# PSUM's eight banks as one pool, one argmax chain per head pair, and a new order of the attention stage

## The chip, the cores and the metric

The kernel runs on one core of one Trainium2 chip. Its time is the device time of that core, in microseconds, from the launch to the end of the last engine. Before the change the median of three runs is 634.14 us (634.08 to 634.79).

## The reference

Three blocks follow each other. Only the first, a clustered attention, is touched by the change; the other two are named since they fill the rest of the time.

```python
# attention: B=2, H=8, S=768, D=64, 16 clusters per head
q_assign = argmax(q_n @ c_n.T)          # cluster of every query (normalised rows)
k_assign = argmax(k_n @ c_n.T)          # cluster of every key
mask = q_assign[:, None] == k_assign[None, :]
scores = where(mask, q @ k.T / 8, -1e9)
attn = exp(scores - max(scores)); attn /= sum(attn) + 1e-9
x = attn @ v                            # heads side by side: (B, S, 512)
# block 2: xk, xr = mixes of x and x shifted by one token
x = sigmoid(xr @ w_r) * (relu(xk @ w_k) ** 2 @ w_v)
# block 3: token mixing, then channel mixing
u = x + (relu(x.T @ w_tok1) @ w_tok2).T
out = u + relu(u @ w_ch1) @ w_ch2
```

## The kernel before

**Tiling.** Heads are worked two at a time: eight pairs, numbered 0 to 7. A pair has 12 tasks: two token halves (hf 0 and 1) of three 128-query tiles for each of the two heads (e 0 and 1). One task is: scores of 128 queries against 768 keys (`score`, four TensorE matmuls of 384 columns, tile `s`, two PSUM banks); the row maximum (`rowmax`, VectorE); the exponential (`expo`, ScalarE, tile `e`); then a turn of `e`, because attn @ v needs keys on the partitions. Tasks of half 0 are turned on TensorE (`transp_p`, six transposes of 128 columns in two groups of three, tile `t`, and two copies out of PSUM by VectorE or ScalarE, `evac_p`); tasks of half 1 are turned in 32x32 blocks on VectorE (`transp_d`) and put in place by 16 DMAs per pair (`shuffle`, tile `ptd`). The product with v (`pv`) is a chain of 12 matmuls for a half, accumulated in one bank (tile `x`; the trace records every such plain float32 matmul twice, so 24 rows a chain); `xevac` scales it by the reciprocal row sums, which `denom`, `recip`, `spread`, `rbcast` (three transposes, tile `rb`) and `rbevac` bring to the right partitions.

**Mask.** While pair n is worked, pair n+1 is prepared: q and k are split into a high and a low part (`hi`, `lo`), and the clusters are found. `sims` multiplies q and k with the centroids; `sime` copies that to SBUF, for each half of the tokens apart (128x384); `simt` turns each half with three TensorE transposes; `amx`, `aeq`, `ark`, `am2`, `aoh` (VectorE, 128x192 each) make a one-hot row of the first maximum; `mask` turns it back (three transposes) and `mske` (ScalarE) scales it. So there are two chains of these steps per pair, one per half. `mdma` then moves the result by four DMAs on SyncE's queue into rows of the q and k operands, where the second part of every score matmul adds it; no score of pair n+1 can start before.

**PSUM.** Eight banks are dealt out by name: `psS` holds two score tiles of two banks each, `psT` two banks for turned tiles, `pair` one bank `m` (sims, masks, row sums) and one bank `x` (the v product, the other half of sims). When attention ends, these pools are closed and six accumulators `a0` to `a5` for the blocks behind take their place, beside `x` and `m`.

**What sets the order.** Within the attention stage a planner in the kernel's own Python code (`Op`, `run_plan`) places every operation. Each `Op` has an engine, an assumed duration, its predecessors, and a due time from the tables `DUE`, `EARLY` (pair 0) and `LATE` (the last pair). At every step the planner takes, over all engines, the ready operation that can start first, with due times as the tie-breaker at a weight of `DUE_W`. On the chip each engine then runs its list strictly in that order. A score op of task g waits in the plan for `exp_` of task g-2, since there are two score tiles. Where TensorE would pause at the start, `fill_x` puts 14 idle transposes. After the attention stage a second scheduler (`Chain`, `pump`) lays out the dense blocks; its rules are not touched.

Of the kernel before, what the change touches and what calls it, by code (L numbers as in the profile page):

```python
# [33 lines left out]
SCALE = 1.0 / math.sqrt(D)  # L34
NSTG = 3
# [21 lines left out]
DUE = {'s': 0.075,  # L57
 'mx': -0.216,
 'ex': 0.934,
 'td': 1.972,  # L60
 'tp0': 2.127,
 'tp1': 1.924,
 'ev0': 2.789,
 'ev1': 2.471,
 'sime0': 3.215,
 'simt0': 3.916,
 'amx0': 3.075,
 'aeq0': 4.244,
 'ark0': 0.056,
 'am20': 5.655,  # L70
 'aoh0': 5.222,
 'mask0': 6.793,
 'mske0': 7.102,
 'sime1': 5.354,
 'simt1': 4.15,
 'amx1': 6.062,
 'aeq1': 3.912,
 'ark1': 3.439,
 'am21': 2.284,
 'aoh1': 4.612,  # L80
 'mask1': 7.092,
 'mske1': 6.0,
 'mdma': 11.061,
 'hi00': 4.779,
 'hi01': 3.762,
 'hi02': 1.798,
 'hi10': -5.56,
 'hi11': 7.343,
 'hi12': 9.268,
 'lo00': 4.909,  # L90
 'lo01': 6.659,
 'lo10': 7.645,
 'lo11': 13.069,
 'loads': 11.015,
 'loadv': 22.198,
 'rcp': 8.118,
 'rbp': 9.821,
 'rep': 12.198,
 'rcd': 12.255,
 'rbd': 13.951,  # L100
 'red': 15.747,
 'pvd': 20.878,
 'pvp': 12.812,
 'xed': 22.451,
 'xep': 13.571,
 'ksp': 0.283,
 'ksd': 0.542,
 'sh': 15.329,
 'sims': 3.038,
 'f0': -2.206,  # L110
 'f1': 1.08,
 'f2': -0.163,
 'f3': 0.286,
 'f4': 0.039,
# [11 lines left out]
EARLY = {0: {'simt1': 6.854,
     'f1': -0.046,
     'lo01': 6.792,
     'lo11': 11.641,
     'amx1': 6.029,  # L130
     'rep': 11.63,
     'sh': 14.421,
     'loadv': 23.651,
     'mske0': 4.694,
     'xed': 22.706,
     'g': 12.575,
     'sime1': 4.215,
     'rcd': 10.132,
     'mask1': 6.301,
     'ark0': 3.08,  # L140
     'f6': -2.983,
     'hi02': 3.667,
     'rcp': 6.686,
     'pvd': 20.92,
     'am20': 5.3,
     'lo00': 5.616,
     'ksp': -0.992,
     'f8': 0.942,
     'loads': 12.84,
     'x1': 10.466,  # L150
     'rbd': 14.022,
     'tp1': 1.876,
     'ksd': 0.54,
     'f9': 1.924,
     'aeq1': 4.212,
     'xep': 12.88,
     'simt0': 2.943,
     'x0': 2.453,
     'ev1': 2.379,
     'mask0': 7.408,  # L160
     'hi01': 3.184,
     'mske1': 6.134}}
# [68 lines left out]
def cluster_attention_moe_mixer(ctx: ExitStack, tc, q, k, v, cent, mu_k, mu_r, w_k, w_v, w_r, w1, w2, wc1, wc2, out):  # L231
# [15 lines left out]
    nc.vector.tensor_copy(identb, ident)  # L247
    rank = const.tile([P, NC], F32, name="rank")
# [271 lines left out]
    with ExitStack() as actx:  # L520
# [4 lines left out]
        pctx = actx.enter_context(ExitStack())  # L525
        psS = pctx.enter_context(tc.tile_pool(name="psS", bufs=2, space=PSUM))
        psT = pctx.enter_context(tc.tile_pool(name="psT", bufs=2, space=PSUM))
# [27 lines left out]
        def prep_steps(n):  # L555
# [29 lines left out]
            def sims():  # L585
                for hf in range(2):
                    st["ps", hf] = pair.tile([P, HS], F32, tag="mx"[hf], name="sims")
                for e in range(2):
                    for j, r in ((0, qr), (1, kr)):
                        o = 32 * (2 * e + j)  # L590
                        for hf in range(2):
                            rows = slice(D * hf, D * hf + D)
                            nc.tensor.matmul(
                                st["ps", hf][o : o + 32, :], cn[rows, 2 * p + e, :],
                                r[e][rows, hf * HS : (hf + 1) * HS], start=True, stop=True,
                            )

            def sims_head(e):
                if e:
                    st["ps", e] = ps = psT.tile([P, HS], F32, tag="t", name="sims")  # L600
                else:
                    st["ps", e] = ps = pair.tile([P, HS], F32, tag="m", name="sims")
# [28 lines left out]
            def sime(hf):  # L631
                sm = sml.tile([P, HS], F32, tag="sm", name="sm")
                nc.scalar.activation(sm, st["ps", hf], AF.Copy)
                st["sm", hf] = sm
# [849 lines left out]
```

## Time and profile before

| | |
|---|---|
| median of 3 runs | 634.14 us (634.08 to 634.79) |
| profiled execution | span 633.0 us from first to last instruction; no own time is listed for it beside the span |
| TensorE busy (PE) | 618.0 us, 98% |
| VectorE busy (DVE) | 484.3 us, 77% |
| ScalarE busy (ACT) | 358.9 us, 57% |
| GpSimd busy (POOL) | 129.2 us, 20% |
| mean granted TensorE clock | 0.995 |

The median lies 1.1 us above the span of the profiled execution. A busy TensorE is not a TensorE at its peak: matmuls are pipelined, and a row's duration holds the time in the pipe, so that rows overlap. What an instruction costs the stream is read from the distance between the start of its row and the start of the next. SPq is SyncE's DMA queue, PEld TensorE's weight loads. In the 40 slices of the page (15.8 us each) attention fills the first 15.

### The profile page before, as it was taken

To read this page: it belongs to the slowest core of one execution; us is meant where nothing else is said; L and a number is where in the kernel's file an instruction comes from. 1 tells how busy PE (TensorE), PEld (TensorE's weight loads), DVE (VectorE), ACT (ScalarE), POOL (GpSimd) and SP (SyncE) were. 2 spreads that over 40 slices of the span, in tenths; PEclk is the share of its full clock that TensorE was granted. 3 is DMA by queue.
4 is the path that set the end of the run, shared out by engine and by line. 5 is a ranking of instruction groups with operands and counts; after the bars stand their busy time and mean duration, and the time that the engine had idled before them with its cause. 6 is when DMAs were issued, how large, how long until landed. Compare 5 with 4: busy or idle time off the path is not lost.

```text
span 633.0 us, 9550 instructions
## 1 busy us (share of the span) xinstructions
PE 618.0 (98%) x3357; PEld 500.5 (79%) x3357; DVE 484.3 (77%) x888; ACT 358.9 (57%) x690; POOL 129.2 (20%) x181
## 2 busy tenths in 40 slices
PE   7899999999999999999999999999999999999997
PEld 5756657566575677899999998888999899999996
DVE  5789898999988955788969889869988635875113
ACT  4878888788886956776748665314443421332110
POOL 4354735547264351000000000020002000000000
PEclk9799999999999999999999999999999999999999
DMA  8156847749574352333312443151446312410002
GB/s 289 63 163 152 240 133 217 209 101 269 167 184 109 80 150 100 100 121 115 126 38 67 133 134 133 36 132 45 157 133 155 100 45 100 133 34 1 1 1 99
DMA packets 36735, 75.43 MB, mean 119 GB/s; under 512 B 6032, under 2 KB 19344, under 8 KB 36688
## 3 DMA queue, kind: packets, MB, share of 16 engines
q1 hardware_dynamic: 34256, 67.36, 34.7%
q0 software_dynamic: 2432, 7.47, 4.9%
q8 instruction: 26, 0.43, 0.3%
q14 instruction: 21, 0.17, 0.1%
HBM read 48.27 MB, written 3.15 MB: 81 GB/s over the span
## 4 chain that ended last, share of the span: by engine, by line
PE 76%; DVE 11%; ACT 5%; issue 3%; DMA 2%; SPq 1%; POOL 0%; DVEq 0%; ACTq 0%; POOLq 0%
PE h L1230 25%; PE acc L1254 24%; PE x L844 8%; PE s L755 6%; PE r L513 5%; DVE junk L763 3%; ACT e L772 3%; DMA uperm<-ublk 2%; PE t L828 2%; SPq L1352 1%; PE tok L1310 1%; ACT ptp L536 1%; PE tok L1393 1%; PE rb L794 1%; DVE ut L1365 1%
## 5 line engine op out<-in xcount | busy, mean ns | idle before, releaser
L1254 PE MATMUL acc<-wu,hl 128*128 128x512 f32 x720 | 170.5, 391 | 0.0
L1254 PEld LDWEIGHTS acc<-wu,hl 128*128 128x128 f32 x720 | 134.6, 188 | 26.8
L1230 PE MATMUL h<-ut,wu 128*128 128x384 f32 x576 | 104.5, 336 | 0.4 <-DVE ut L1365 0.3
L772 ACT ACTIVATE e<-s,nm 128x768 f32<-128x768 f32 x96 | 86.5, 902 | 29.8 <-DVE junk L763 26.6
L1230 PEld LDWEIGHTS h<-ut,wu 128*128 128x128 f32 x576 | 100.9, 188 | 3.0 <-DVE ut L1365 0.8
L763 DVE TENSOR_SCALAR_CACHE_REDUCE junk<-s 128x768 bf16<-128x768 f32 x96 | 90.4, 942 | 13.3 <-PE s L755 12.4
L1209 ACT ACTIVATE hl<-h 128x384 fp32r<-128x384 f32 x48 | 23.5, 491 | 93.7 <-PE h L1230 93.7
L1211 DVE SCALAR_TENSOR_TENSOR hl<-h,hl 128x384 fp32r<-128x384 f32 x48 | 26.7, 557 | 60.0 <-ACT hl L1209 59.6
L406 ACT ACTIVATE wu<-g 128x512 fp32r<-128x512 f32 x62 | 39.1, 630 | 55.9 <-DVE g L402 55.9
L1230 PE MATMUL h<-xmix,wu 128*128 128x384 f32 x384 | 69.2, 335 | 0.0
L1230 PEld LDWEIGHTS h<-xmix,wu 128*128 128x128 f32 x384 | 67.3, 188 | 1.1
L755 PE MATMUL s<-ka,qa 128*128 128x384 f32 x192 | 59.3, 391 | 3.1 <-ACT e L772 2.6
L1352 POOL DMA_DIRECT2D uperm<-ublk x16 | 7.9, 500 | 229.5 <-ACT h L1297 169.1
L755 PEld LDWEIGHTS s<-ka,qa 128*128 128x128 f32 x192 | 29.5, 193 | 29.9 <-ACT e L772 21.0
L755 PE MATMUL s<-kb,qb 80*128 80x384 f32 x192 | 50.1, 343 | 0.9 <-POOL kb L538 0.9
L408 DVE TENSOR_TENSOR wu<-g,wu 128x512 fp32r<-128x512 f32 x58 | 40.5, 698 | 13.1 <-ACT wu L406 11.4
L402 DVE SCALAR_TENSOR_TENSOR g<-wu,g 128x512 f32<-128x512 f32 x62 | 42.8, 690 | 4.5
L807 DVE STREAM_TRANSPOSE tb<-e 128x768 f32<-128x768 f32 x48 | 45.8, 959 | 0.0
L390 DVE SCALAR_TENSOR_TENSOR g<-wraw,g 128x512 uint32<-128x512 uint32 x62 | 42.7, 689 | 1.1
L828 PE MATMUL t<-ident,e 128*128 128x128 f32 x288 | 42.6, 281 | 0.7 <-DVE ptp L534 0.3
L396 DVE SCALAR_TENSOR_TENSOR g<-wraw,g 128x512 uint32<-128x512 uint32 x62 | 42.4, 684 | 0.2
L828 PEld LDWEIGHTS t<-ident,e 128*128 128x128 f32 x288 | 34.7, 144 | 7.9 <-issue 3.6
(112 smaller groups left out, 879.4 us busy)
## 6 DMA issues: line engine op xcount, KB each, us to landing
wraw<-moe_w_ch_dram SPq DMA_DIRECT2D x34, 512.0 KB, 3.5
ptd<-tb SPq DMA_DIRECT2D x88, 144.0 KB, 4.2
t<-q_dram SPq DMA_DIRECT2D x16, 384.0 KB, 4.4
t<-k_dram SPq DMA_DIRECT2D x16, 384.0 KB, 4.7
ptd<-tb POOLq DMA_DIRECT2D x40, 144.0 KB, 4.3
wraw<-moe_w_k_dram SPq DMA_DIRECT2D x9, 512.0 KB, 3.3
wraw<-moe_w_v_dram SPq DMA_DIRECT2D x9, 512.0 KB, 3.9
v<-v_dram SPq DMA_DIRECT2D x8, 384.0 KB, 3.8
```

The source lines that it names most:

```text
L390: nc.vector.scalar_tensor_tensor(out=g, in0=high, scalar=0xC0000000, in1=g, op0=ALU.bitwise_and, op1=ALU.bitwise_or)
L396: nc.vector.scalar_tensor_tensor(out=g, in0=low, scalar=29, in1=g, op0=ALU.logical_shift_right, op1=ALU.bitwise_or)
L402: nc.vector.scalar_tensor_tensor(out=gf, in0=f32(t[:, 1, :]), scalar=TINY, in1=gf, op0=ALU.is_ge, op1=ALU.mult)
L408: (nc.gpsimd if key[0] == "wr" else nc.vector).tensor_tensor(out=t[:, 1, :], in0=gf, in1=f32(t[:, 0, :]), op=ALU.subtract)
L755: nc.tensor.matmul(ps[:, nh, 0:HS], x[:, e, c0 : c0 + P], y[:, e, nh * HS : (nh + 1) * HS], start=first, stop=not first,)
L763: nc.vector.tensor_scalar(junk, PS_[t][:, :, 0:HS], -SCALE, None, op0=ALU.mult, op1=ALU.min, accum_out=nm)
L772: nc.scalar.activation(et.rearrange("p (a b) -> p a b", a=2), PS_.pop(t)[:, :, 0:HS], AF.Exp, bias=NM_.pop(t), scale=SCALE, accum_out=ss_[ ...
L807: nc.vector.transpose(out=T_[n][:, :, e, :, i, :].rearrange("p j k q -> p k j q"), in_=E_.pop(t).rearrange("p (k j c) -> p k j c", j=4, c=32),
L828: nc.tensor.transpose(ps[:, kk], E_[t][:, kt * P : (kt + 1) * P], ident)
L844: nc.tensor.matmul(o, vts[n][:, e, kt, :], m, start=(kt == 0), stop=(kt == NT - 1))
L1230: nc.tensor.matmul(ps[:, 0:HS], u[:, wl, c, :], xin(xl, c, sl), start=(n == 0), stop=(n == 11))
L1254: nc.tensor.matmul(accs[st], prev[:, xl, st * P : (st + 1) * P], u[:, wl, :], start=(idx == 1 and n == 0), stop=(idx == nf and n == 2),)
```

## The change

1. One PSUM tile `banks8` of eight banks replaces the four pools. An `Op` now says how many banks it needs (`need`) and which earlier operations' banks its end gives back (`frees`); `pick_banks` chooses the bank, and `start` makes an op wait for one. Scores take any even-odd pair of banks, single tiles any bank. The wait of a score for `exp_` of task g-2 and the waits by name of bank are gone; which operation waits for which is decided by the planner through the banks.
2. The two argmax chains per pair become one over both token halves: `sime`, `amx` to `aoh`, `mask` and `mske` run once per pair on twice the size. `simt` is no longer a transpose of 128 columns but a matmul of the same weights with `pick`, 64 columns of the identity, so that only the 16 used columns of each group of 32 are written.
3. In pair 0 the five argmax steps and one mask copy, which were one operation or stood ahead of the plan, become operations of the plan.
4. All due times are set anew, many far outside the pair (-218, 202), and with them the order on every engine. `fill_x` has no predecessor any more.
5. Behind the attention stage the six accumulators and the two small banks keep whichever banks the plan left them (`home`).

TensorE, in the second half of a pair in steady state (before: pair 2 to pair 3): the v products (`x`) of the pair before and of this pair, the scores (`s`, each task two rows `ka` and `kb`), the row sums (`rb`).

```order
L844 MATMUL x<-ptd,v_270 64x384 x4
L755 MATMUL s<-ka_635,qa_633 128x384 x2
L755 MATMUL s<-kb_636,qb_634 128x384 x2
L844 MATMUL x<-ptd,v_270 64x384 x2
L755 MATMUL s<-ka_938,qa_936 128x384 x2
L755 MATMUL s<-kb_939,qb_937 128x384 x2
L844 MATMUL x<-ptp,v_940 64x384 x4
L755 MATMUL s<-ka_938,qa_936 128x384 x2
L755 MATMUL s<-kb_939,qb_937 128x384 x2
L844 MATMUL x<-ptp,v_940 64x384 x6
```

The same place of the program after the change; every PSUM tile is called `ps` now.

```order
L843 MATMUL ps<-ptd,v_949 64x384 x4
L754 MATMUL ps<-ka_870,qa_868 128x384 x2
L754 MATMUL ps<-kb_871,qb_869 128x384 x2
L754 MATMUL ps<-ka_870,qa_868 128x384 x2
L754 MATMUL ps<-kb_871,qb_869 128x384 x2
L843 MATMUL ps<-ptd,v_949 64x384 x8
L843 MATMUL ps<-ptp,v_1121 64x384 x2
L754 MATMUL ps<-ka_1169,qa_1167 128x384 x2
L754 MATMUL ps<-kb_1170,qb_1168 128x384 x2
L793 MATMUL ps<-ident,rw 128x128 x3
```

Stretches of v matmuls are longer and fewer, and two tasks' scores stand next to each other between them. Over the whole stage the v products stand in 25 stretches where they stood in 46, and the scores in 80 where they stood in 93.

VectorE, at the argmax of the coming pair, before: the two chains with the row maxima (`junk`) between.

```order
L647 TENSOR_REDUCE mx<-simsT 128x12
L650 TENSOR_TENSOR simsT<-simsT,mx 128x12x16
L656 TENSOR_TENSOR simsT<-simsT,rank 128x12x16
L763 TENSOR_SCALAR junk,nm<-s 128x768
L662 TENSOR_REDUCE m_1466<-simsT 128x12
L665 TENSOR_TENSOR oh<-simsT,m_1466 128x12x16
L763 TENSOR_SCALAR junk,nm<-s 128x768
L647 TENSOR_REDUCE mx<-simsT 128x12
L650 TENSOR_TENSOR simsT<-simsT,mx 128x12x16
L656 TENSOR_TENSOR simsT<-simsT,rank 128x12x16
L662 TENSOR_REDUCE m_1509<-simsT 128x12
L665 TENSOR_TENSOR oh<-simsT,m_1509 128x12x16
```

And after:

```order
L633 TENSOR_REDUCE mx<-ps 128x24
L636 TENSOR_TENSOR ps<-ps,mx 128x384
L641 TENSOR_TENSOR ps<-ps,rank 128x384
L762 TENSOR_SCALAR junk,nm<-ps 128x768
L647 TENSOR_REDUCE m_1299<-ps 128x24
L762 TENSOR_SCALAR junk,nm<-ps 128x768
L650 TENSOR_TENSOR oh<-ps,m_1299 128x24x16
```

Ten operations have become five of twice the size, with two row maxima among them.

TensorE, at the start, before: the masks of pair 1 are turned, then the 14 idle transposes (`fill`), the first row sums and scores.

```order
L673 LDWEIGHTS oh
L673 MATMUL ohT<-identb,oh 128x128
L1000 MATMUL fill<-ident 128x128 x14
L794 MATMUL rb<-ident,rw 128x128 x3
L755 MATMUL s<-ka_200,qa_198 128x384 x2
```

After, the 14 transposes stand right behind the second part of the first two score tasks, ahead of the second masks of pair 0 (`oh`).

```order
L754 MATMUL ps<-kb_194,qb_192 128x384 x4
L1027 MATMUL ps<-ident 128x128 x14
L754 MATMUL ps<-ka_193,qa_191 128x384 x2
L754 MATMUL ps<-kb_194,qb_192 128x384 x2
L692 LDWEIGHTS oh
```

They have moved from the middle of pair 0's work to its beginning, and a third score task has moved ahead of those masks.

```diff
+NBANK = 8
+NEXP = 4
...
-DUE = {'s': 0.075,
- 'mx': -0.216,
...
+DUE = {'s': -0.396,
+ 'mx': 1.598,
...
+    pick = ident.rearrange("p (a b) -> p a b", b=32)[:, :, 0:NC]
...
-    pair = ctx.enter_context(tc.tile_pool(name="pair", bufs=1, space=PSUM))
-    turn = [0]
-
-    def bank(name):
+    psum = ctx.enter_context(tc.tile_pool(name="psum", bufs=1, space=PSUM))
+    banks8 = psum.tile([P, NBANK, 512], F32, name="ps")
+    turn, home = [0], {}
+
+    def bank(*_):
         turn[0] ^= 1
-        return pair.tile([P, 512], F32, tag="xm"[turn[0]], name=name)
+        return banks8[:, home["xm"[turn[0]]]]
...
-        psS = pctx.enter_context(tc.tile_pool(name="psS", bufs=2, space=PSUM))
-        psT = pctx.enter_context(tc.tile_pool(name="psT", bufs=2, space=PSUM))
...
+            def sime():
+                st["sm"] = sm = sml.tile([P, S], F32, tag="sm", bufs=1, name="sm")
+                nc.scalar.activation(sm.rearrange("p (h s) -> p h s", h=2), st["ps"], AF.Copy)
+
+            def simt(at):
+                ps = banks8[:, at, 0 : NT * 4 * NC].rearrange("p (i c) -> p i c", i=NT)
+                for i in range(NT):
+                    nc.tensor.matmul(ps[:, i], st["sm"][:, i * P : (i + 1) * P], pick, start=True, stop=True)
+                st["sv"] = ps.rearrange("p i (a b) -> p (i a) b", b=NC)
...
+            def aeq():
+                nc.vector.tensor_tensor(
+                    out=st["sv"], in0=st["sv"], in1=st["mx"].unsqueeze(2).to_broadcast([P, NT * 4, NC]), op=ALU.is_ge
+                )
...
+            def mask(at):
+                st["pm"] = ps = banks8[:, at].bitcast(BF16)[:, 0:S]
+                for i in range(NT):
                     nc.tensor.transpose(
-                        ps[:, i].rearrange("p a b -> p (a b)"), st["sm", hf][:, i * P : (i + 1) * P], ident
+                        ps[:, i * P : (i + 1) * P], oh[i // HT][:, i % HT].rearrange("p a b -> p (a b)"), identb
                     )
...
+            def mske():
+                nc.scalar.activation(mst, st["pm"], AF.Identity, bias=mbi, scale=msc)
...
-                PS_[t] = psS.tile([P, 2, 512], F32, tag="s", name="s")
+                PS_[t] = banks8[:, at : at + 2]
...
+        free_at = [0.0] * NBANK
+
+        def pick_banks(need, t):
+            if need == 2:
+                spots = [(max(free_at[i], free_at[i + 1]), i) for i in range(0, NBANK, 2)]
+                return min((max(f, t), i) for f, i in spots)
+            return min((max(f, t), free_at[i ^ 1] <= max(f, t), -i) for i, f in enumerate(free_at))
...
+                if o.need:
+                    t = pick_banks(o.need, t)[0]
...
+                for h in o.frees:
+                    h.holders -= 1
+                    h.until = max(h.until, o.end + CROSS)
+                    if not h.holders:
+                        for i in range(max(h.need, h.kept)):
+                            free_at[h.at + i] = h.until
...
-                score_[g] = Op("P", 0.7 if g > 1 else 0.35, want(n, "s", j), lambda t=t, g=g: score(t, None if g > 1 else 1),
-                               parts[n][e] + [mask_dma.get(n), exp_.get(g - 2), score_.get(g - 1)], tail=0.2)
+                score_[g] = Op("P", 0.7 if g > 1 else 0.35, want(n, "s", j), lambda *at, t=t, g=g: score(t, None if g > 1 else 1, *at),
+                               parts[n][e] + [mask_dma.get(n), score_.get(g - 1), q6 if n == 0 and hf else None], tail=0.2, need=2 if g > 1 else 0)
...
-                for f in range(2):
-                    o = Op("A", 0.41, want(n, f"sime{f}"), act(f"sime{f}"), [si, simt_.get((n - 1, f))])
-                    o = simt_[n, f] = Op("P", 0.33, want(n, f"simt{f}"), act(f"simt{f}"), [o], tail=0.2)
...
+                o = Op("A", 0.77, want(n, "sime"), act("sime"), [si, simt_.get(n - 1)], frees=[si])
+                t = o = simt_[n] = Op("P", 0.66, want(n, "simt"), act("simt"), [o], tail=0.2, need=1)
+                for x, us in (("amx", 0.55), ("aeq", 0.52), ("ark", 0.4), ("am2", 0.5), ("aoh", 0.4)):
+                    o = Op("D", us, want(n, x), act(x), [o, mask_.get(n - 1) if x == "aoh" else None], frees=[t] if x == "aoh" else [])
+                mask_[n] = Op("P", 0.4, want(n, "mask"), act("mask"), [o], tail=0.2, need=1)
+                e0 = Op("A", 0.87, want(n, "mske"), act("mske"), [mask_[n], mask_dma.get(n)], frees=[mask_[n]])
+                mask_dma[p] = Op("S", 2.0, want(n, "mdma"), act("mdma"), [e0, last_score(n - 1)], kb=192)
...
-                x_free = [Op("P", 0.109 * FILL_X, want(0, "s", 9.9), fill_x, x_free)]
+                fx = Op("P", 0.109 * FILL_X, want(0, "s", 9.9), fill_x, need=1)
+                fx.frees = [fx]
```

The numbers in the `Op` calls are the planner's assumptions, not measurements.

## Rows read from the trace of the kernel before

**Rows 1.** Busy time by stretch: start:end, length, then each engine's busy us, granted clock

```profile
core 0: us, PE busy (x) PEld busy (x) DVE busy (x) ACT busy (x) POOL busy (x), PEclk, DMA share, GB/s
...
45.90:74.50 28.60, 27.71 (x177) 17.92 (x176) 25.66 (x55) 23.51 (x49) 16.36 (x19) 1.00 0.69 195
...
101.20:127.40 26.20, 25.66 (x167) 16.70 (x167) 23.69 (x51) 21.35 (x45) 11.38 (x14) 1.00 0.72 209
127.40:154.00 26.60, 25.99 (x174) 16.86 (x182) 25.51 (x54) 22.03 (x46) 14.21 (x16) 1.00 0.61 173
...
180.40:242.40 62.00, 61.40 (x355) 39.85 (x355) 46.66 (x90) 43.43 (x83) 27.24 (x30) 1.00 0.44 112
242.40:633.00 390.60, 386.11 (x1916) 346.11 (x1914) 277.95 (x463) 173.90 (x320) 9.74 (x17) 1.00 0.29 91
```

**Rows 2.** Waits in total: who waited, for whom, us, times, longest

```profile
PEld s L755 <- ACT e L772: 21.0, 41, 1.3
```

**Rows 3.** Timeline of TensorE, one pair: start us, us, instruction, count

```profile
103.11 0.49 PE L639 MATMUL simsT<-ident,sm 128*128 128x128 f32 x3
103.44 0.49 PE L828 MATMUL t<-ident,e 128*128 128x128 f32 x3
...
104.80 0.82 PE L828 MATMUL t<-ident,e 128*128 128x128 f32 x6
105.39 0.61 PE L755 MATMUL s<-ka,qa 128*128 128x384 f32 x2
...
106.19 0.82 PE L828 MATMUL t<-ident,e 128*128 128x128 f32 x6
...
116.00 0.62 PE L755 MATMUL s<-ka,qa 128*128 128x384 f32 x2
...
116.90 0.87 PE L844 MATMUL x<-ptd,v 128*64 128x384 f32 x4
117.69 0.62 PE L755 MATMUL s<-ka,qa 128*128 128x384 f32 x2
```

**Rows 4.** Timeline of TensorE: two score tasks next to each other

```profile
86.46 0.52 PE L755 MATMUL s<-ka,qa 128*128 128x384 f32 x2
...
87.17 0.49 PE L794 MATMUL rb<-ident,rw 128*128 128x128 f32 x3
```

**Rows 5.** Timeline of TensorE: one whole v product without a break

```profile
221.51 4.09 PE L844 MATMUL x<-ptp,v 128*64 128x384 f32 x24
225.53 5.06 PE L513 MATMUL r<-wu,xmix 128*128 128x512 f32 x21
```

**Rows 6.** Timeline of VectorE: a row maximum and one argmax chain

```profile
106.61 0.95 DVE L763 TENSOR_SCALAR_CACHE_REDUCE junk<-s 128x768 bf16<-128x768 f32 x1
...
107.48 0.35 DVE L647 TENSOR_REDUCE mx<-simsT 128x12 f32<-128x192 f32 x1
...
109.13 0.36 DVE L665 TENSOR_TENSOR oh<-simsT,m 128x192 bf16<-128x192 f32 x1
109.41 0.95 DVE L763 TENSOR_SCALAR_CACHE_REDUCE junk<-s 128x768 bf16<-128x768 f32 x1
```

**Rows 7.** The queue of SyncE at the mask, and its DMAs' KB and us to landing

```profile
112.56 0.59 SPq L687 DMA_DIRECT2D kb<-mst  x1
...
kb<-mst SPq DMA_DIRECT2D x14, 48.0 KB, 2.1
```

**Rows 8.** Timeline of TensorE at the start, and the fill

```profile
12.61 0.94 PE L755 MATMUL s<-kb,qb 80*128 80x384 f32 x4 [0.92 <-POOL kb L538]
14.94 0.84 PE L693 MATMUL ohT<-identb,oh 128*32 128x128 bf16 x12 [1.40 <-DVE oh L624]
...
32.40 1.70 PE L1000 MATMUL fill<-ident 128*128 128x128 f32 x14
33.94 0.49 PE L794 MATMUL rb<-ident,rw 128*128 128x128 f32 x3
```

**Rows 9.** Busy time by stretch, at the start, columns as in rows 1

```profile
16.20:23.00 6.80, 6.16 (x23) 5.97 (x24) 4.84 (x11) 5.32 (x13) 0.82 (x1) 0.50 0.40 129
```

More of the change, by code (lines that the diff above doesn't have):

```diff
@@ L56 @@
 DUE_W = 0.29
-DUE = {'s': 0.075,
- 'mx': -0.216,
[L59 to L105, printed above, removed]
+DUE = {'s': -0.396,
+ 'mx': 1.598,
+ 'ex': 2.613,
+ 'td': 4.497,
+ 'tp0': 1.698,
+ 'tp1': -113.403,
+ 'ev0': 3.66,
+ 'ev1': 4.432,
+ 'sime': -36.319,
+ 'simt': 4.842,
+ 'amx': 5.794,
+ 'aeq': -184.185,
+ 'ark': -101.081,
+ 'am2': 7.867,
+ 'aoh': 8.538,
+ 'mask': 9.134,
+ 'mske': 11.214,
+ 'mdma': -80.13,
+ 'hi00': 6.93,
+ 'hi01': -88.971,
+ 'hi02': 14.795,
+ 'hi10': -115.954,
+ 'hi11': 9.687,
+ 'hi12': -30.273,
+ 'lo00': 61.261,
+ 'lo01': 11.338,
+ 'lo10': 64.182,
+ 'lo11': 82.204,
+ 'loads': 102.466,
+ 'loadv': -115.258,
+ 'rcp': 3.831,
+ 'rbp': 12.361,
+ 'rep': 44.098,
+ 'rcd': 7.485,
+ 'rbd': 13.734,
+ 'red': -2.826,
+ 'pvd': 21.443,
+ 'pvp': 12.229,
+ 'xed': 35.918,
+ 'xep': -92.475,
  'ksp': 0.283,
  'ksd': 0.542,
- 'sh': 15.329,
- 'sims': 3.038,
- 'f0': -2.206,
+ 'sh': -81.725,
+ 'sims': -75.301,
+ 'f0': -32.547,
  'f1': 1.08,
- 'f2': -0.163,
- 'f3': 0.286,
- 'f4': 0.039,
+ 'f2': -60.217,
+ 'f3': -218.06,
+ 'f4': -10.943,
  'f5': -0.601,
@@ L136 @@
      'g': 12.575,
[L137 to L140, printed above, removed]
+     'sime': 5.794,
+     'rcd': -35.891,
+     'mask': -43.146,
      'f6': -2.983,
[L142 to L146, printed above, removed]
+     'hi02': 84.047,
+     'rcp': -70.725,
+     'pvd': 22.259,
+     'lo00': -57.145,
      'ksp': -0.992,
-     'f8': 0.942,
-     'loads': 12.84,
+     'f8': -85.204,
+     'loads': 76.584,
      'x1': 10.466,
-     'rbd': 14.022,
@@ L583, in lo, with sims @@
                 eng.tensor_tensor(out=dst, in0=src, in1=f32(h), op=ALU.subtract)
-            def sims():
-                for hf in range(2):
-                    st["ps", hf] = pair.tile([P, HS], F32, tag="mx"[hf], name="sims")
+            def sims(at):
+                st["ps"] = banks8[:, at : at + 2, 0:HS]
                 for e in range(2):
@@ L598, in sims_head @@
             def sims_head(e):
[L599 to L602, printed above, removed]
+                st["ps", e] = ps = banks8[:, (6, 5)[e], 0:HS]
                 for hf in range(2):
@@ L629, in aoh_head, with sime_head @@
                 )
[L631 to L634, printed above, removed]
-            def simt(hf):
-                ps = pair.tile([P, HT, 4, 32], F32, tag="mx"[hf], name="simsT")
-                for i in range(HT):
+            def sime_head(e):
+                if e == 0:
+                    st["sm"] = sml.tile([P, S], F32, tag="sm", bufs=1, name="sm")
+                st["sm", e] = sm = st["sm"][:, e * HS : (e + 1) * HS]
+                nc.scalar.activation(sm, st["ps", e], AF.Copy)
@@ L743, in is_d, with score @@
             return hf == 1
-        def score(t, part=None):
+        def score(t, part=None, at=None):
             n, hf, i, e = t
```

343 lines of the change are left out of this document (170 added, 173 removed).

## The prediction

> **What bounds the kernel now.** I read the busy time by stretch first [rows 1]. Everything behind 242.4 us is the dense part: TensorE is busy 386.1 of 390.6 us there, and the change leaves its instructions as they are, so I carry it over. What can move lies ahead of 242.4. From pair to pair (stretches cut at the `sims` of two neighbouring pairs) attention takes 26.2 and 26.6 us; TensorE shows 25.7 and 26.0 of these as busy, VectorE 23.7 and 25.5. So two engines are nearly full: a gain needs both to have less to do or fewer waits between them. ScalarE (21.4 and 22.0) and GpSimd (11.4 and 14.2) have room.
>
> TensorE's busy share flatters it, since rows overlap. I therefore priced its stream by the distances between starts in one pair's timeline [rows 3 to 5]:
> - A score task costs 0.80 us before transposes (105.39 to 106.19), 0.90 before a v stretch (116.00 to 116.90), and 0.71 as the second of two neighbouring tasks (86.46 to 87.17).
> - A v stretch of 4 rows costs 0.79 (116.90 to 117.69), the unbroken chain of 24 rows 4.02 (221.51 to 225.53). The line through both is 0.1615 per row and 0.144 for leaving the stretch. Entering cost the score 0.10, so one stretch more or less is worth 0.24.
> - Six transposes cost 0.59 (104.80 to 105.39), three `simt` ones 0.33 (103.11 to 103.44).
>
> Summed over a pair before, with my estimates of 0.81 for `sims` and 1.2 for masks and row sums: 12 scores 10.1, 48 v rows in six stretches 8.6, 36 transposes 3.7, `simt` 0.66; together 25.1. Measured is 26.5 on average, so about 1.4 us of a pair is stall. Part of it is the score that waits for a score bank: the row of waits shows weight loads of scores waiting 21.0 us in 41 waits for exponentials [rows 2], not all of it on the path, since loads run ahead of the matmuls.
>
> **Fewer stretches on TensorE.** The order shows 25 v stretches for 46, about three a pair for six: 3 x 0.24 = 0.72 us less per pair. Two score tasks a pair stand right behind another instead of one: 0.1 less (0.71 for 0.80). Together 0.8.
>
> **simt as a plain matmul.** Six transposes (0.66) become six plain float32 matmuls with the same weights and 64 columns. No row shows that shape. From below: priced by columns against the transposes, 0.33. From above: the v products show two rows per plain float32 matmul (24 rows for 12 instructions) [rows 5], so 12 passes at a transpose's 0.11 make 1.32. I take 1.05, nearer to the top, since two passes are seen and weights load for each. That is +0.4 per pair (-0.33 to +0.66).
>
> The row first: 42 `simt` transposes of this kernel cost 0.11 each [rows 3]. The Trainium skill (TensorE: Matmul & The Clock Gate, Terms) says that float32 runs four times faster in transpose mode than without; half the columns at four times the price would be twice 0.66, so 1.32 per pair and, by the rule, a result some 1.8 us later over seven pairs than with my value. Here the two rows per matmul agree with more than one pass, and no run yet shows the shape.
>
> **The argmax on VectorE.** The second chain takes 1.93 us from its first start to the next row maximum (107.48 to 109.41), of which the last step takes 0.28 (109.13 to 109.41), when an independent instruction follows [rows 6]. Two chains: 3.86. A row maximum of 768 elements takes 0.87 (106.61 to 107.48), so (0.87-0.28)/576 = 1.02 ns per further element. A step of 384 elements then costs 0.28+0.20 = 0.48 before an independent instruction and 0.41+0.20 = 0.61 before one that needs its result (107.48 to 109.13 is 1.65 for four). With the new order two of the five are of the dear kind: 2x0.61+3x0.48 = 2.7. VectorE saves 1.2 us a pair (bounds: 0, if each step costs twice the old, and 1.9, if size were free). `sime` and `mske` also lose one start each on ScalarE, some 0.2 a pair, at nothing, since ScalarE idles 4 us a pair. Alone, VectorE's saving isn't worth its own size: it shortens what TensorE waits for.
>
> **Stalls.** I walked one steady pair of the new order by hand with these durations. The banks are taken as planned, so scores no longer wait for the task two before. Two stalls stay: the last transposes of half 0 wait for an exponential that sits behind the argmax steps, and the score task after them takes the banks that `aoh` frees. Together I get 0.8 us, and TensorE's own sum of 24.7 (25.1-0.8+0.4), so 25.5. A hand walk forgets small latencies; I give 0.3 back and take 1.1 of stall for 1.4. The bounds are 0 and 2.1. What is late next is the argmax chain itself.
>
> **Added wait.** Both halves' mask now hangs on one chain. Behind `mdma` SyncE's queue holds the next q and k loads, v and the 11 shuffles, and TensorE's first score of the next pair waits. Before, the last of four issues starts at 112.56 and lands 2.1 later, so 114.7, and the next pair's first score starts at 117.69: 3.0 slack [rows 3, 7]. In my walk 1.2 remain, so I cost it at nothing; if the chain comes later than that, each pair pays the excess.
>
> **The start.** TensorE ran at the granted clock 0.50, that is 1.2 GHz, from 16.2 to 23.0 us [rows 9]; ahead of the fall it had little to do: it waited 0.92 before 12.61 and 1.40 before 14.94 [rows 8]. The fill (1.54, 32.40 to 33.94) now stands where it waited, so it is free there and leaves pair 0's middle. If the clock stays full, TensorE does these 6.2 us in 3.1, but VectorE is busy 4.84 of the 6.8, so at most 2.0 come back; the first row maximum starts later, as argmax steps stand ahead of it. I take -1.0, between -2.0 and +1.5 (the clock falling elsewhere, where nothing covers it: half of 6.8 is 3.4 lost, less the 2.0 it costs now).
>
> **Sum.** Per pair -0.8 (stretches) +0.4 (simt) -0.3 (stalls) = -0.7. Seven pairs whose work holds the preparation of a next one, and the last pair with its stretches but no argmax: 7 x 0.7 + 0.6 = 5.5. The slow pair of 28.6 us holds the same parts and 2 us more stall [rows 1]; I take 0.4 of it. With the start 1.0 the sum is -6.9. Against the span of 633.0 that is 626.1; the median lies 1.1 above, so 627.2.
>
> **Rivals.**
> 1. *Slower: the single argmax chain decides.* Place: last argmax step, mask turn, `mske`, four mask DMAs, first score of the next pair. For it: the chain now ends once, late, with two row maxima inside, and the masks stand behind two more scores. Against it: 1.2 us slack in the walk. It costs from the point where the chain slips by 1.2, and it makes the kernel slower from 1.2+0.7 = 1.9. With a slip of 2.6 (a row maximum and a turn more on VectorE, 0.95 each, and `simt` at its upper bound, 0.66) a pair takes 0.7 more than before; seven pairs and the start at -1.0 give +3.9: 638.0.
> 2. *No gain: VectorE is the bound.* It is busy 25.5 of 26.6 in one stretch [rows 1]. If its argmax steps cost twice the old, TensorE's savings turn into waits for row maxima: only the start's gain stays, 633.1.
> 3. *Stalls go altogether.* With all eight banks shared, TensorE runs at its own sum of 24.7: 1.8 less a pair, 12.6 in seven, and 2 at the start: 619.5. For it: waits for score banks are the largest in the list [rows 2]. Against it: three engines stay within a few us of each other in the first half of a pair.
> 4. *Small gain.* simt at 1.32 (+0.27 a pair) and no stall recovered (+0.3): 7 x 0.57 = 4.0 less gain, 631.2.
> That the dense part changes is unlikely: its banks are the same in number.
>
> **Chances.** The forecast (623 to 629.5) 0.52, small gain (629.5 to 632.8) 0.16, stalls gone (below 623) 0.14, no change 0.08, slower 0.10. What a measurement can tell from no change is 0.2%, here 1.3 us. So faster 0.82, same 0.08, slower 0.10. The range leaves out the far ends of the third and the first rival: 619.5 to 634.5; the forecast's own range is 623 to 629.5.
>
> **What would show it.** Right: distances between `sims` of neighbouring pairs near 25.8 where they were 26.2 to 26.6; three v stretches a pair; five argmax steps taking 2.7; weight loads of scores waiting far less for exponentials; granted clock 1.00 between 16 and 23 us; the dense part 390.6 as before. The `simt` group tells its price directly: more than 1.3 a pair, and the gain shrinks. Wrong: first scores of a pair waiting for mask DMAs (rival 1), TensorE waiting for row maxima at pair distances above 26 (rival 2), or a dense part that changes by more than 1 us.

## The result, and the profile after

The changed kernel takes 627.63 us (median, 626.43 to 629.22) where the kernel before, on the same chip, takes 634.32: ratio 0.9897, 95% interval 0.9881 to 0.9914. Predicted were 627.2. The profiled execution took 628.16, its span 626.4, so 6.6 less than before's span of 633.0. The total agrees; the parts don't, and this section shows where. One execution further down, of the kernel with later loads, ran at a lower granted clock (660.55 us, clock 0.982); it stands in no range or ratio here.

Attention's end is read first. Behind the last v product TensorE goes on with `xr @ w_r` of block 2. That row started at 242.38 before and starts at 235.34 now: 7.0 were won ahead of it, and the dense part from there on takes 391.06 for 390.62. The busy time by stretch of the changed kernel, cut at sims (columns as in rows 1):

```profile
92.69:118.01 25.32, 25.07 (x175) 17.77 (x173) 22.94 (x45) 20.34 (x41) 14.12 (x17) 1.00 0.69 185
118.01:145.09 27.08, 25.89 (x175) 17.98 (x173) 22.77 (x45) 21.30 (x42) 14.11 (x17) 1.00 0.76 203
145.09:170.33 25.24, 24.99 (x174) 17.76 (x172) 22.94 (x45) 20.71 (x42) 12.87 (x16) 1.00 0.68 178
...
235.34:626.40 391.06, 386.12 (x1916) 346.15 (x1914) 278.61 (x464) 173.63 (x321) 11.61 (x19) 1.00 0.29 91
```

Two pairs take 25.3 where before took 26.2 and 26.6 [rows 1], and one of the same work between them takes 27.1. The difference stands in sims itself, in TensorE's timeline (start us, us, instruction, count, and the idle time before a row with its releaser):

```profile
23.56 0.88 PE L583 MATMUL ps<-t,cn 64*32 64x384 f32 x16
...
118.01 1.02 PE L583 MATMUL ps<-t,cn 64*32 64x384 f32 x12
119.96 0.84 PE L583 MATMUL ps<-t,cn 64*32 64x384 f32 x4 [0.94 <-DMA t<-k_dram]
...
170.33 0.86 PE L583 MATMUL ps<-t,cn 64*32 64x384 f32 x12
172.91 0.84 PE L583 MATMUL ps<-t,cn 64*32 64x384 f32 x4 [1.71 <-DMA t<-k_dram]
```

Undisturbed it takes 0.88, as in every pair before. Here the last four of its sixteen rows wait for a load of k. Over seven pairs sims takes 5.6 longer than 0.88 each (0.06, 0.53, 0.33, 1.91, 0.26 and 2.54 from the second pair on). The totals of the waits name the same load, and show that the wait on which I had looked is nearly gone (21.0 in 41 waits before [rows 2]):

```profile
PEld ps L754 <- ACT e L771: 2.5, 5, 0.7
...
PEld ps L583 <- DMA t<-k_dram: 4.6, 4, 2.4
PE ps L583 <- DMA t<-k_dram: 2.7, 2, 1.7
```

The timeline of SyncE's queue shows why the loads are late:

```profile
111.32 0.59 SPq L686 DMA_DIRECT2D kb<-mst  x1
112.01 0.51 SPq L537 DMA_DIRECT2D t<-q_dram  x1
...
113.60 0.37 SPq L537 DMA_DIRECT2D t<-k_dram  x1
```

and the chain of waits has two of these loads on it, start and length:

```profile
113.60 6.32 DMA t<-k_dram
165.14 7.73 DMA t<-k_dram
```

They stand behind the mask DMAs, as before. But before, the loads issued from 113.27 to 115.22 were needed at 127.39, twelve us later. The last of them on SyncE's queue, and sims in TensorE's timeline, before the change:

```profile
114.85 0.37 SPq L546 DMA_DIRECT2D t<-k_dram  x1
127.39 0.88 PE L593 MATMUL sims<-t,cn 64*32 64x384 f32 x16 [0.16 <-ACT rb L536]
```

The new order has sims ahead of the pair's third and fourth score, where it stood behind them, and scores earlier throughout: sims starts at 118.01 where it started at 127.39, while the loads are issued only 1.3 earlier. The one issued at 113.60 lands at 119.92; its four rows would start at about 118.6.

To see what each part of attention gained, I compare the start of the eighth score task of each pair (both orders have the same scores in the same sequence; us, from the timelines; "early loads" is the first experiment):

| | pair 0 | 1 | 2 | 3 | 4 | 5 | 6 | 7 | attention's end |
|---|---|---|---|---|---|---|---|---|---|
| before | 29.40 | 54.17 | 80.55 | 107.17 | 133.60 | 160.15 | 186.38 | 211.37 | 242.38 |
| after | 27.75 | 51.10 | 77.51 | 102.83 | 129.75 | 155.16 | 182.70 | 205.05 | 235.34 |
| early loads | 27.67 | 50.99 | 77.39 | 102.39 | 127.45 | 152.61 | 177.62 | 199.97 | 230.40 |

Up to pair 1 3.1 are won, from there to pair 2 nothing, from pair 2 to 6 only 0.6 in four pairs, in pair 7, which has no sims, 2.6, and 0.7 behind it.

### The profile page after: what moved, and what is told of

Read it like the earlier page. It is cut to its first block, busy times and chain, and to the rows that moved or that the text cites. A ratio compares the mean times of both kernels' runs of the same rounds, so it can differ in the third digit from the quotient of the medians.

```text
span 626.4 us, 9596 instructions
## 1 busy us (share of the span) xinstructions
PE 610.4 (97%) x3399; PEld 505.4 (81%) x3399; DVE 484.1 (77%) x863; ACT 353.0 (56%) x666; POOL 128.7 (21%) x181
## 4 chain that ended last, share of the span: by engine, by line
PE 81%; DVE 5%; DMA 4%; ACT 4%; issue 3%; SPq 2%; POOL 1%; DVEq 0%; ACTq 0%; POOLq 0%
PE ps L1250 25%; PE ps L1274 25%; PE ps L754 10%; PE ps L843 8%; PE ps L827 4%; DMA t<-k_dram 3%; PE ps L507 2%; PE ps L628 1%; PE ps L1330 1%; ACT e L771 1%; PE ps L583 1%; PE ps L1413 1%; PE ps L793 1%; DMA uperm<-ublk 1%; SPq L1372 1%
## 5 line engine op out<-in xcount | busy, mean ns | idle before, releaser
L1274 PE MATMUL ps<-wu,hl 128*128 128x512 f32 x720 | 170.5, 391 | 0.0
L1274 PEld LDWEIGHTS ps<-wu,hl 128*128 128x128 f32 x720 | 134.6, 188 | 26.8
L1250 PE MATMUL ps<-ut,wu 128*128 128x384 f32 x576 | 104.4, 336 | 0.2 <-DVE ut L1385 0.2
L1250 PEld LDWEIGHTS ps<-ut,wu 128*128 128x128 f32 x576 | 101.0, 188 | 2.4 <-DVE ut L1385 0.7
L771 ACT ACTIVATE e<-ps,nm 128x768 f32<-128x768 f32 x96 | 86.7, 906 | 26.2 <-DVE junk L762 23.4
L762 DVE TENSOR_SCALAR_CACHE_REDUCE junk<-ps 128x768 bf16<-128x768 f32 x96 | 90.3, 940 | 11.5 <-PE ps L754 9.3
L1250 PE MATMUL ps<-xmix,wu 128*128 128x384 f32 x384 | 69.4, 335 | 0.6 <-DVE wu L399 0.6
L1250 PEld LDWEIGHTS ps<-xmix,wu 128*128 128x128 f32 x384 | 67.2, 188 | 2.0 <-DVE wu L399 1.0
L754 PE MATMUL ps<-ka,qa 128*128 128x384 f32 x192 | 56.4, 375 | 3.4 <-POOL kb L529 1.4
L754 PE MATMUL ps<-kb,qb 80*128 80x384 f32 x192 | 49.6, 340 | 0.9 <-DVE qb L698 0.9
```

Source lines behind the costliest of these rows:

```text
L754: nc.tensor.matmul(ps[:, nh, 0:HS], x[:, e, c0 : c0 + P], y[:, e, nh * HS : (nh + 1) * HS], start=first, stop=not first,)
L762: nc.vector.tensor_scalar(junk, PS_[t][:, :, 0:HS], -SCALE, None, op0=ALU.mult, op1=ALU.min, accum_out=nm)
L771: nc.scalar.activation(et.rearrange("p (a b) -> p a b", a=2), PS_.pop(t)[:, :, 0:HS], AF.Exp, bias=NM_.pop(t), scale=SCALE, accum_out=ss_[ ...
L1250: nc.tensor.matmul(ps[:, 0:HS], u[:, wl, c, :], xin(xl, c, sl), start=(n == 0), stop=(n == 11))
L1274: nc.tensor.matmul(accs[st], prev[:, xl, st * P : (st + 1) * P], u[:, wl, :], start=(idx == 1 and n == 0), stop=(idx == nf and n == 2),)
```

## The experiments

Each kernel is the changed one with one edit, or the one with early loads with one edit, timed against the kernel before (634.4 to 634.6 in these runs).

**Early loads.** The load that overwrites a buffer is issued behind that buffer's last reader and the pair's shuffles (`read` is called by sims, hi and lo for q, j=0, and k, j=1; `moved_` counts the shuffles issued on SyncE's queue; the helper that holds the last two lines is written out here):

```
     def loads(n):
+        if n < 2:
...
+    def read(n, e, j):
+        readers[n, e, j] = readers.get((n, e, j), 0) + 1
+        if 1 <= n < NP - 1 and readers[n, e, j] == (3, 4)[j]:
+            owed.append((n + 1, e, j))
+        while owed and (owed[0][0] < 3 or moved_[0] >= 11 * (owed[0][0] - 2)):
+            load(*owed.pop(0))
```

> The changed kernel with one thing altered: each q and k load of the pair after next is issued as soon as the last reader of the buffer it overwrites stands in the program (behind the pair's shuffles), on the same queue, so ahead of the four mask DMAs and no longer behind them; the orders of TensorE, VectorE, ScalarE and GpSimd are unchanged. Theory A (sims waits for late q and k loads: in the trace of the changed kernel its sixteen matmuls take 0.02 to 2.6 us longer than the 0.86 of an undisturbed one, 5.7 us in seven pairs): sims takes 0.86 in every pair and the time falls by 3.5 to 5.7, to 622 to 624. Theory B (the loads are slow by bandwidth, or the mask DMAs, pushed back by about 1.3 us, make the first mask score of the next pair wait): the waits stay or move to the scores, 626 to 630.

Measured: 624.28 (623.74 to 624.88), ratio 0.9841 (0.9828 to 0.9854), clear of the changed kernel's interval and 3.4 less by the medians, just under the 3.5 to 5.7 of theory A. TensorE's timeline of it, and SyncE's queue:

```profile
142.78 0.88 PE L600 MATMUL ps<-t,cn 64*32 64x384 f32 x16
143.59 0.62 PE L773 MATMUL ps<-ka,qa 128*128 128x384 f32 x2
```

```profile
107.60 0.33 SPq L535 DMA_DIRECT2D t<-k_dram  x1
108.28 0.51 SPq L705 DMA_DIRECT2D qb<-mst  x1
```

Sims takes 0.88 in all pairs. From pair 2 to 6 the profiled execution takes 100.23; the changed kernel's 105.19 less its four waits at sims there (5.04) is 100.15. So these waits are the whole difference between the two profiled executions there, and theory A holds. Attention ends 4.9 earlier; 0.5 of it is given back in the dense part (391.6). The mask DMAs, now behind the loads, hardly matter: TensorE's matmuls wait 0.3 for them in all.

**Early loads on GpSimd's queue.**

```
-                load(*owed.pop(0))
+                load(*owed.pop(0), nc.gpsimd)
```

> As the run with early loads, but these loads are issued from GpSimd's queue right behind their last reader there, so that the mask DMAs on the other queue aren't pushed back. Theory A: 622 to 624, below the variant on the shared queue if that one makes mask scores wait. Theory B (bandwidth): 626 to 629. A cost of its own: four issues of about 0.5 us a pair on GpSimd, which idles 5 us there, so nothing.

Measured: 629.03 (ratio 0.9917, 0.9905 to 0.9930): a miss. Sims takes 0.88 here too, so the loads come in time, but the gain is lost elsewhere. Its timeline of TensorE, totals of waits and list of DMAs (KB, median us to landing):

```profile
89.58 0.62 PE L773 MATMUL ps<-ka,qa 128*128 128x384 f32 x2
90.81 0.59 PE L773 MATMUL ps<-kb,qb 80*128 80x384 f32 x2 [0.60 <-DMA kb<-mst]
```

```profile
PE ps L773 <- DMA kb<-mst: 2.9, 3, 1.3
```

```profile
kb<-mst SPq DMA_DIRECT2D x14, 48.0 KB, 3.8
```

TensorE now waits 2.9 for mask DMAs, of the 4.8 that are lost against the loads on SyncE's queue: they land 3.8 after their issue (2.1 in the changed kernel), while the last load, issued just ahead of them, is under way. Each issue also takes GpSimd 0.56, and 0.30 before it; what share of the rest that has was not separated. My "nothing" had left out both. This is the place of my first rival, reached by another way.

**simt as transposes again.**

```
-   for i in range(NT): nc.tensor.matmul(ps[:, i], st["sm"][:, i*P:(i+1)*P], pick, start=True, stop=True)
+   for i in range(NT): nc.tensor.transpose(raw[:, i % 4], st["sm"][:, i*P:(i+1)*P], ident)
```

> The changed kernel with the six plain matmuls of simt (64 columns each) made six transposes of 128 columns again, in the same place of the same order. Two blocks are overwritten in the bank, so the argmax reads other values and the masks are of other tokens; all shapes and counts stay. Trace of the changed kernel: simt takes 1.25 to 1.28 us a pair; six transposes should take 0.6 to 0.66. Theory A (simt's price lies on TensorE's path): 0.6 in each of seven pairs, -4.2, so 623.4. Theory B (in pairs where sims then waits for its loads the time saved turns into a longer wait): under -2, so 626 to 627.6.

Measured: 622.96 (622.13 to 629.34), ratio 0.9845 (0.9813 to 0.9876). TensorE's timeline in the changed kernel, then in this one:

```profile
125.26 1.45 PE L628 MATMUL ps<-ident,sm 128*128 128x64 f32 x12
126.52 0.60 PE L754 MATMUL ps<-ka,qa 128*128 128x384 f32 x2
```

```profile
122.30 0.82 PE L629 MATMUL ps<-ident,sm 128*128 128x128 f32 x6
122.88 0.60 PE L755 MATMUL ps<-ka,qa 128*128 128x384 f32 x2
```

From start to start 1.26 against 0.58: 0.68 a pair, 4.8 in seven, and the medians differ by 4.7. That these agree doesn't show that the whole price lies on the path. The means of the two kernels differ by 3.6, and the executions of this one scatter over 7.2. In its profiled execution sims also waits less for its loads, 2.8 in seven pairs where the changed kernel waits 5.6. Less these waits, pair 2 to 6 takes 98.30 against 100.15, so 0.46 a pair. Theory A holds for about two thirds of simt's price; the rest of what the profiled execution gained in these pairs is shorter waits at sims.

**No fill at the start**, once with late loads and once with early ones.

```
-   for _ in range(FILL_X): nc.tensor.transpose(banks8[:, at, 0:P], ident, ident)
+   pass
```

> The changed kernel without the 14 fill transposes (13.39 to 14.84 in its trace), order otherwise the same. Theory A (they keep TensorE's granted clock at 1.00 from 16 to 23 us): the clock falls to 0.50 somewhere behind 14 us and pair 0 takes 1 to 3 us longer, 628.5 to 630.5. Theory B (the clock stays at 1.00 without them, or VectorE bounds pair 0 anyway): within 1 us of 627.6, or 1 us less if the fill is not hidden.

> The kernel with early loads, without the 14 fill transposes at the start. Without them in the kernel with late loads sims of pair 0 came 0.64 later (24.20 for 23.56) and the granted clock of 16.2 to 23.0 us was 0.75 for 1.00, but the time stayed (627.4 for 627.6). Theory A (late loads covered the loss): here it shows, +0.5 to +1.0, 624.8 to 625.3. Theory B (something else of pairs 0 and 1 takes it up): 624.3, within 0.3.

Measured: 627.39 (0.9901, 0.9885 to 0.9916) and 624.67 (623.16 to 625.5; 0.9845, 0.9830 to 0.9859): neither differs from its counterpart by more than the scatter. The clock does. Stretches of the changed kernel, and of the one with late loads and no fill:

```profile
16.20:23.00 6.80, 4.73 (x40) 4.33 (x41) 5.82 (x14) 5.41 (x12) 0.82 (x1) 1.00 0.27 108
```

```profile
16.20:23.00 6.80, 5.42 (x35) 4.78 (x36) 5.81 (x13) 5.01 (x11) 0.82 (x1) 0.75 0.25 91
```

With the 14 transposes the granted clock is 1.00 (2.4 GHz), without them part of the stretch is at 1.2 GHz (0.75, and 0.61 with early loads). In the profiled execution with early loads sims of pair 0 comes 2.4 later without them, and the delay stays up to pair 7; but other executions of that kernel were up to 2.3 us shorter than the profiled one. So that the fill holds the clock is shown, its worth in time is not settled: 0.4 by the medians, inside a scatter of 2.3.

**Similarities on 64 rows** (code shortened).

```
-   matmul(st["ps"][32*(2*e+j) : +32, hf], cn[rows, 2*p+e, :], ..., start=True, stop=True)
+   matmul(st["ps"][32*e : +32, hf], cnz[rows, 32*(2*p+e) + NC*(1-j) : +32], ..., start=j == 0, stop=j == 1)
-   matmul(ps[:, i], sm[:, i*P:(i+1)*P], pick, ...)
+   transpose(ps[:, i], sm[0:64, i*P:(i+1)*P], ident[0:64, 0:64])
```

> The kernel with early loads, and sims written compactly: q and k of a head share 32 output rows (two accumulated matmuls, the other half of the weights is zero), so the similarities stand on 64 rows, and simt is six transposes of 64 columns in one bank instead of six plain matmuls. The result is the reference's. All counts and the orders stay. Theory A (simt lies on TensorE's path and transposes cost by their columns, 0.33 to 0.66 for six where the plain ones take 1.26): 0.6 to 0.9 less in each of seven pairs, so 618 to 620 where the early loads alone gave 624.3. Theory B (the plain matmul is dear because of its shape and the 64-column transposes cost 0.2 each too, or other engines take up the gain): 622 to 624.3.

Measured: 624.5 (0.9844, 0.9831 to 0.9857), no gain over the early loads. TensorE's timeline:

```profile
143.89 1.51 PE L602 MATMUL ps<-t,cn 64*32 64x384 f32 x16
145.33 0.62 PE L775 MATMUL ps<-ka,qa 128*128 128x384 f32 x2
...
149.94 0.58 PE L649 MATMUL ps<-ident,sm 64*128 64x64 f32 x6
150.45 0.62 PE L775 MATMUL ps<-ka,qa 128*128 128x384 f32 x2
```

simt falls to 0.51 as hoped, but the sixteen rows of sims take 1.44 where they took 0.81 from start to start. They now write two groups of 32 rows and no longer four, and they also sum in pairs; which of the two costs was not separated. Neither theory had this.

**Scores that wait for the exponential of two before.** A 32x32 transpose ahead of the score reads that exponential (code shortened); the control has the same transposes reading the one of four before (the first control had them at 92 scores, the second at the same 75):

```
+   et = E_done[g - 2]        # controls: g - 4
+   nc.tensor.transpose(banks8[0:32, at, HS:HS+32], et[0:32, S-32:S], ident[0:32, 0:32])
```

> The kernel with early loads, and ahead of a score task one 32x32 transpose that reads the exponential of the task two before (where that one stands earlier in the program, 75 of 94 scores), into unused columns of the score's bank: in the new order TensorE waits for what two score banks would make it wait for. Against it the next run, whose extra transposes read the exponential of four before. Theory A (the prediction: the pool gives back little, 0.3 a pair): 2 to 4 above the next run. Theory B (the new order lives on more than two score pairs in flight, and nearly all of the 1.4 of stall a pair went through it): 8 to 15 above.

> As the run before, but the extra transposes (92) read the exponential of the task four before, which has long ended, so they cost their own time alone: 0.03 to 0.11 each by the 128-column ones, 3 to 10 in all, if nothing covers them: 627 to 634. Under both theories it is the control for the run before.

> The exact control for the run with waits on the exponential of two before: the same 75 extra transposes in the same places, reading the exponential of four before. The 92 of the first control cost 19.7 over the kernel with early loads, 0.214 each, so 75 cost 16.1: 640.4, and the wait for the exponential of two before is worth 646.3 less this. Theory A (the prediction: the pool gives back 0.3 a pair): this run comes out at 643 to 645. Theory B (nearly all of the 1.4 of stall a pair went through the two score pairs): at 631 to 638. By the arithmetic between: 640.4, 0.75 a pair.

Measured: 646.27, 644.0 and 640.4 (ratios 1.0200, 1.0180 to 1.0219; 1.0155, 1.0141 to 1.0169; 1.0104, 1.0089 to 1.0118). The first control cost 0.214 per transpose, far above the 0.03 to 0.11 that I expected, and had more of them, so that it told little; the second landed on its forecast. The wait is worth 646.27 less 640.40, 5.9 us or 0.74 in each of eight pairs: between the two theories. By the eighth scores of the profiled executions it is 0.89 in each pair from 2 to 6 (28.19 for 27.29) and nothing in pair 7 (24.88 and 24.89), where the transposes alone slow a task from 1.36 to 1.69. Only 75 of the 94 scores can be made to wait so: the others stand ahead of that exponential in the new order, so this is not all that two score tiles would cost. The waits for exponentials in the first kernel, and in its second control:

```profile
PEld ps L769 <- ACT e L796: 20.1, 32, 2.0
```

```profile
PEld ps L769 <- ACT e L796: 8.0, 16, 0.6
```

The 20.1 is near the 21.0 of the kernel before [rows 2], and it shows what such a row is worth on the path: it stands 12.1 above the control's, and the time 5.9, half of that.

**Later loads.** Four tiny DMAs stand behind the mask DMAs on the queue:

```
+   for e in range(4): nc.sync.dma_start(out=spare[:, e], in_=f32(mst[32*e : 32*e+NC, 0:16]))
```

> The changed kernel with four small DMAs (16 by 16 numbers each, read by nobody) between the mask DMAs and whatever follows them on the queue, so the next q and k loads are issued about 2.2 later in each of six pairs. Theory A (sims stands waiting for these loads, most of the pairs without slack): 1.5 to 2.5 more in five or six pairs, +8 to +14, so 636 to 642 and slower than the kernel before. Theory B (the waits at sims were covered by other waits of the pair, and the early loads gained through something else, as less crowding of the DMA engines): under +4, below 632.

Measured: 652.3 (650.59 to 654.42), ratio 1.0281 (1.0265 to 1.0298): theory A, but well beyond its 636 to 642. TensorE's timeline, one sims in three pieces:

```profile
132.61 1.51 PE L584 MATMUL ps<-t,cn 64*32 64x384 f32 x8
134.79 0.83 PE L584 MATMUL ps<-t,cn 64*32 64x384 f32 x4 [0.66 <-DMA t<-q_dram]
137.03 0.83 PE L584 MATMUL ps<-t,cn 64*32 64x384 f32 x4 [1.40 <-DMA t<-k_dram]
```

This sims takes 5.25, 4.4 above 0.88. The four DMAs take the queue 2.5 each time, the loss is 24.7, or 4.1 in each of six pairs. Most of it stands at sims itself, which takes 27.6 longer than undisturbed over the pairs, where it took 5.6 longer. Why a delay of 2.5 costs 4.1 was not separated: the loads now run into the sixteen shuffles, whose median landing rises from 4.7 to 6.8 on SyncE's queue and from 5.1 to 8.6 on GpSimd's.

## Why the prediction came out right, step by step

That the total came out right is luck: errors of both signs cancelled. By the eighth scores, forecast and measured gains are these. Up to pair 1: 1.7 and 3.1. Pair 1 to 2: 1.1 and 0.0. Pair 2 to 6: 2.8 and 0.6. From there to attention's end: 1.3 and 3.4. Dense part: 0 and -0.4. Together: 6.9 and 6.6.

- **Stretches: right.** TensorE's timeline of one pair:

```profile
133.35 1.51 PE L843 MATMUL ps<-ptd,v 128*64 128x384 f32 x8
...
136.41 2.80 PE L843 MATMUL ps<-ptd,v 128*64 128x384 f32 x16
139.04 0.81 PE L843 MATMUL ps<-ptp,v 128*64 128x384 f32 x4
...
141.71 3.45 PE L843 MATMUL ps<-ptp,v 128*64 128x384 f32 x20
145.09 1.14 PE L583 MATMUL ps<-t,cn 64*32 64x384 f32 x16
```

  Three stretches. The last takes 3.38 from start to start; my line (0.1615 a row and 0.144) gives 3.37. No run took this edit alone.
- **simt: too cheap.** 1.26, not 1.05; with a price of 0.66 before, +0.6 a pair. The rule of the Trainium skill (TensorE: Matmul & The Clock Gate, Terms) gave 1.32, and the trace agrees with it within 5% in time. It doesn't bear out the reason: a row of the v product, 384 columns wide, costs 0.16, only 1.5 times the 0.105 of a simt row of 64 columns, so these prices don't go by columns. My bound from above, twelve rows at the price of a transpose, gives the same 1.32 without it. I should have taken that end.
- **The argmax on VectorE: right.** Its timeline:

```profile
126.74 0.56 DVE L633 TENSOR_REDUCE mx<-ps 128x24 f32<-128x384 f32 x1 [0.46 <-PE ps L628]
...
127.94 0.57 DVE L641 TENSOR_TENSOR ps<-ps,rank 128x384 f32<-128x384 f32 x1
128.41 0.95 DVE L762 TENSOR_SCALAR_CACHE_REDUCE junk<-ps 128x768 bf16<-128x768 f32 x1
129.28 0.55 DVE L647 TENSOR_REDUCE m<-ps 128x24 f32<-128x384 f32 x1
129.88 0.96 DVE L762 TENSOR_SCALAR_CACHE_REDUCE junk<-ps 128x768 bf16<-128x768 f32 x1
130.76 0.55 DVE L650 TENSOR_TENSOR oh<-ps,m 128x384 bf16<-128x384 f32 x1
131.23 0.18 DVE L781 RECIPROCAL rs<-ss 128x6 f32<-128x6 f32 x1
```

  1.20 for two steps, then 0.47, 0.60 and 0.47: 2.74, where I had worked out 2.7.
- **Stalls: this step failed.** I left 1.1 of 1.4 a pair, by a walk by hand that I then padded. With early loads a pair takes 25.06 (100.23 in four). My own sum for TensorE, with simt at its measured price, is 24.9; so some 0.15 of stall is left. Of the 1.25 that went, 0.74 to 0.89 hang on scores no longer waiting for the exponential of two before, if the number with early loads holds for before too. The remaining 0.4 to 0.5 (joint argmax, order) was not separated.
- **The last pair: a gain that I had not seen.** From pair 6's eighth score to attention's end 3.4 are won, where I had 1.3. A score and its six transposes stand 1.36 to 1.37 apart there (199.59, 200.95, 202.31, 203.68), where before it was 1.64 to 1.93 (206.23, 207.91, 209.55, 211.37, 213.30). No idle time is noted at these rows of before; only the distances show the stall. It may be the same wait, but the run with added waits can't tell: in pair 7 its control is as slow. The rows show one thing more. Before, ScalarE worked without a break there, and block 2's `t` and `xmix` stood among its exponentials, so that these came late (its timeline, and a piece of the chain of waits):

```profile
208.49 0.92 ACT L772 ACTIVATE e<-s,nm 128x768 f32<-128x768 f32 x1
...
209.36 0.87 ACT L468 ACTIVATE xmix<-t 128x768 fp32r<-128x768 f32 x1
210.17 0.90 ACT L772 ACTIVATE e<-s,nm 128x768 f32<-128x768 f32 x1
```

```profile
211.16 0.83 ACT t L459
```

  In the new order ScalarE has none of these between 198 and 211, and its exponentials follow each other at 1.36:

```profile
201.62 0.90 ACT L771 ACTIVATE e<-ps,nm 128x768 f32<-128x768 f32 x1
...
202.98 0.90 ACT L771 ACTIVATE e<-ps,nm 128x768 f32<-128x768 f32 x1
```

  What moving them gave, and what the banks gave, was not separated; no run tested it.
- **The loads: a step that was missing.** Under the added wait I looked at what mdma releases, and named the q and k loads among what stands behind it, but only the next first score as waiting. That sims had moved two scores nearer to these loads stood in the order. It costs 5.6 in the profiled execution. From pair 2 to 6 it is 5.04, all that the stalls gave there (four times 1.25). With the loads early the same change would have come out near 624, the low end of my forecast's own range.
- **The mask DMAs: right.** The trace shows no wait of TensorE for them; rival 1 did not come. It does in the run with loads on GpSimd's queue.
- **The start: too small.** Up to the eighth score of pair 1 3.1 are won, where I had 1.0 and 0.7 for a pair's gain. 1.65 of it are there by pair 0's eighth score, and the clock is 1.00 in 16 to 23 as forecast. The next 1.4 stand where the fill (1.54) [rows 8] was taken out. I had seen that it was free in its new place, but not added its time at the old one in full.
- **The slow pair: wrong.** From pair 1 to 2 before took 26.38, after 26.41, and 26.40 with early loads; I had 1.1 less (0.7 and 0.4). There was no slow pair to begin with: the 28.6 between two sims [rows 1] hold thirteen score tasks (46.74 to 72.78), not twelve, and 26.38 is like the other pairs. The v rows lie in four stretches there, not three, but before they lay in seven; what took this pair's gain was not separated.
- **Dense part: right** within 0.5 (391.06 for 390.62).

Rival 2 (VectorE the bound) is out: five argmax steps take 2.74, far from twice the old, and VectorE's busy time in a pair fell to 22.9, from 23.7 and 25.5 [rows 1]. Rival 3's mechanism is what happened inside the pairs; the late loads hid it.

## What to carry to other kernels

When an order is set anew, list for each consumer that moved earlier the loads it reads, and take the distance from issue to use in both orders; a load that had 12 us of slack here had less than none. Price an engine's stream by distances between starts: a stall of 0.3 per task shows neither as idle time nor in a busy share of 98%. And when a sum comes out right, check its terms: here a wait of 5.6 us was hidden in a forecast that had hit, and queueing four DMAs earlier in a pair took it out (3.4 by the medians).

## What the runs showed of the hardware

- Sixteen 64x32 matmul rows of 384 columns take 0.81 when their outputs lie in four groups of 32 rows, 1.44 when they lie in two and sum in pairs; which of the two costs is not shown.
- Plain float32 matmuls of 64 columns cost 0.105 for each of two rows per matmul, no less than a transpose of 128 columns (0.097 each, six in 0.58). Transposes of 64 rows and 64 columns cost 0.085 (six in 0.51): the smaller size brings little. A single 32x32 transpose ahead of a score adds 0.214 on average (92 of them, 644.0 for 624.28).
- 48 KB mask DMAs land 2.1 after issue where the q and k loads stand behind them, 2.6 and 2.9 (into k's and q's operands) where they stand ahead on the same queue, 3.8 and 3.4 with a load of 384 KB issued from GpSimd's queue just ahead.
- The kernels whose sims waits for loads scatter over 2.8 us (changed), 3.5 (no fill) and 7.2 (simt as transposes), that with early loads over 1.1 and its variant without fill over 2.3. That the wait makes the scatter is not shown: the kernel with early loads and waits for exponentials scatters over 3.4.
